# Attention and MoE scores in the two row halves of TensorE, without rounded or padded copies

## The chip, the cores and the metric

One Trainium2 chip, one NeuronCore of it. The metric is the time of one execution on the device in microseconds (us); where a kernel ran several times, the median is given. TensorE does matrix products into PSUM (eight banks); VectorE (DVE), ScalarE (ACT) and GpSimd (POOL) do the element-wise work; SyncE (SP) issues most of the transfers.

## The reference

Sliding-window attention (window 128) with a linear position bias is followed by a layer in which four single-head causal attentions act as experts, and each token mixes two of them. B, H, S, D = 8, 8, 576, 64; the model width is 512; there are 4 experts of head width 64.

```python
scores = scale * np.matmul(q, k.transpose(0, 1, 3, 2))
scores = np.where((rel >= 0) & (rel < 128), scores + bias[None], -1e9)
attn = softmax(scores); x = np.matmul(attn, v)          # x as (B, S, 512)
logits = x @ w_gate                                     # two of four experts, w = softmax over the two
for e in range(4):
    q = x @ wq[e]; k = x @ wk[e]; v = x @ wv[e]
    a = softmax(causal(scale * (q @ k.transpose(0, 2, 1))))
    out += gate[e] * ((a @ v) @ wo[e])
```

Inputs and output are fp32. In the kernel a product that has to be nearly fp32 is made in one of two ways: as an fp32 matmul, which the trace shows as two passes of each instruction, or as several matmuls on `float32r` (f32r) operands, a rounded number and the rest that rounding left (high and low part), each of which is one pass.

## The kernel before

**Work.** There are 32 attention groups: a batch of 8 with 4 pairs of heads each. For a group the scores of each head are made in blocks of 128 queries against the two key blocks that the window reaches (the first query block needs one), and the last 64 queries of both heads together as a tail (`attn_s`). VectorE merges the two key blocks under a mask, adds the bias and finds the row's extreme; ScalarE takes the exponential and sums; the blocks are scaled (`normalise`, on GpSimd or ScalarE), transposed on TensorE (`attn_t`), spread by VectorE and multiplied with v (`attn_pv`, `attn_pv_tail`: fp32, the two heads in the two column halves of TensorE). Per batch, x is then multiplied with the weights of q and k (`qkproj`: 12 f32r matmuls of 288 columns for each of 8 outputs) and of v and the gate (`vproj`); for each of two pairs of experts come causal scores in blocks of 128 queries against 128 to 512 keys (`moe_s`), a tail of 64 queries of both experts (`moe_s_tail`), scaling (`moe_norm`), transposes (`moe_t`), products with v (`moe_pv`, again two column halves) and the output product (`moe_wo`).

**Scores before.** Groups 0 to 5 (`n32` = 6) use the raw fp32 q and k: head 0 lies on partitions 0 to 63, head 1 on 64 to 127, and a matmul of 64 rows for each goes to its own row half of TensorE and its own bank (tile `e`). From group 6 on, a rounded copy `h` is brought in by a GpSimd transfer that casts (`load_hi`), the raw copy `r` by SyncE, and four GpSimd subtractions of 64 partitions x 576 make the low parts (`prep`, into `h` and `klA`); a block is then two f32r matmuls over all 128 rows, `s<-h` and `s<-klA,h`, for each head. The other half of the rows holds the low part of q, or padding. The MoE scores are the same: `QSm` holds the high part of q on one half of the rows and the low part on the other, `KHm` the high part of k on both (a transfer from SBUF to SBUF copies it over), `KLm` the low part beside zeros; an eviction of `qkproj` is two casts and two subtractions on 64 partitions each. A block is two matmuls, `ms<-KHm,QSm` and `ms<-KLm,QSm`, for each expert.

**Order.** Every operation is recorded first. A planner (`graph`, `ranks`, `schedule`, `plan`) then sets one fixed order for each engine: a list scheduler with a cost for each operation, ranks by the longest way to the end, and a table `off` in `K` that shifts the rank of each kind of tile in each phase. It charges for changing between row- or column-halved and full matmuls on TensorE, and puts a filling matmul (`warm`) where TensorE would be idle early on. On the chip each engine works through its list in order and waits where an operand is late.

**Buffers.** Scores lie in two PSUM banks (`ps_s`), transposes in two (`ps_t`), qk, v and o in two (`ps_a`), and the products with v in one bank each for attention and MoE.

**Names.** `s`: attention scores, `ms` and `msl`: MoE scores and their tail, `t`, `mt`, `mtl`: transposes, `x`, `xt`, `ma`, `mal`: products with v, `qk`, `v`, `o`: projections. All instructions carry line 1220, where the recorded list is issued; so they are told apart by tile.

Of the kernel before, what the change touches and what calls it, by code (L numbers as in the profile page):

```python
# [78 lines left out]

# [68 lines left out]
def _pairs(ops):  # L148
    two = {}
    for i in range(1, len(ops)):  # L150
        e, m, a, k = ops[i]
        if e != "tensor" or m != "matmul" or a[1].dtype != F32:
            continue
        x = a[0] if a[0].ap[0][1] == D else a[1]
        if x.ap[0][1] == D and x.offset // x.ap[0][0] >= D:
            assert ops[i - 1][0] == "tensor"
            two[i - 1] = i
    return two


def graph(ops, alt):
    n = len(ops)
    raw = _depend(ops)
    two = _pairs(ops)
    rep = list(range(n))
    for a, b in two.items():
        rep[b] = a
# [18 lines left out]
    alts = [[(ENG.index(o[0]), _cost(*o)) for o in alt.get(i, [ops[i]])] for i in nodes]  # L186
    port = [[_port(*o) for o in alt.get(i, [ops[i]])] for i in nodes]
# [4 lines left out]
    kind = []  # L192
    for i in nodes:
        e, m, a, k = ops[i]
        if e != "tensor":
            kind.append(0)
        elif i in two or (m == "matmul" and a[1].ap[0][1] == D):
            kind.append(3)
        elif m == "matmul" and a[1].dtype == F32R:
            kind.append(1)  # L200
        else:
            kind.append(2)
# [15 lines left out]
SWITCH = (150, 45)  # L218
# [5 lines left out]
def ranks(g):  # L224
# [15 lines left out]
    for i in reversed(topo):  # L240
        c = g["cost"][i] + (20 if g["kind"][i] == 3 else 0)
# [11 lines left out]
def schedule(g, rank, succ, setup=0.0, wt=0.5, bias=((0, 0, 0, 0, 0),) * 2, fill=(900, 60000, 9999), cw=6, hs=0):  # L253
    mode = 0
# [21 lines left out]
    while done < n:  # L276
# [97 lines left out]
def plan(ops, alt):  # L374
# [8 lines left out]
    for x in order:  # L383
# [6 lines left out]
        if i in g["two"]:  # L390
            out.append(ops[g["two"][i]])
# [13 lines left out]
class _Rec:  # L405
    def __init__(self):
# [3 lines left out]
        self.alt = {"hold": {}, "early": set()}  # L410
# [7 lines left out]
def attn_moe_kernel(ctx, tc, hd, rd, vd, wall, wo, mk, tb, tm, mt, ident, out):  # L418
# [4 lines left out]
    raw = ctx.enter_context(tc.tile_pool(name="raw", bufs=1))  # L423
# [49 lines left out]
    mkt = cp.tile([P, P + D], I32, name="mkt")  # L473
    tbt = cp.tile([P, NP_, 5, P], BF16, name="tbt")
# [14 lines left out]
    KLA = [cp.tile([P, 2, S], F32R, name=f"klA{k}") for k in range(2)]  # L489

    QW = S + TAIL
    HW = 2 * QW + 2 * S

    N32 = K["n32"]
    EK = QW

# [4 lines left out]
    def load_e(g):  # L501
# [806 lines left out]
```

## Time and profile before

| | |
|---|---|
| median of 3 runs | 582.44 us (580.57 to 585.34) |
| span of the profiled execution, first to last instruction | 583.1 us |
| TensorE busy, matmuls | 562.3 us |
| VectorE, ScalarE, GpSimd busy | 404.3, 420.0, 352.4 us |
| granted TensorE clock, mean | 0.991 |
| moved by DMA | 80.38 MB |

The profile gives no other time for the profiled execution than its span; it lies among the times of the runs, 0.7 us over their median. A matmul's busy time overlaps with that of the next one, since matmuls are pipelined; so what a matmul takes of TensorE is read here from one start to the next. An fp32 matmul stands in the trace as two records, its two passes.

### The profile page before, as it was taken

How to read it: one execution, taken by the hardware profiler on the slowest of the kernel's cores; microseconds unless marked ns; L12 is line 12 of the kernel's file. 1: busy time of each engine (PE TensorE's matmuls, PEld its weight loads, DVE VectorE, ACT ScalarE, POOL GpSimd, SP SyncE). 2: the span in 40 equal slices, each digit the busy share in tenths (PEclk: the TensorE clock that was granted, in tenths of full speed). 3: DMA queues.
4: the chain of work that ended last, by engine and by line, in shares of the span. 5: the costliest groups of instructions: out<-in, count | busy, mean ns of one | idle time of the engine just before them, and what ended most of it. 6: DMA issues, size and time to landing. Idle time of an engine off the chain costs nothing.

```text
span 583.1 us, 14004 instructions
## 1 busy us (share of the span) xinstructions
PE 562.3 (96%) x4565; PEld 477.2 (82%) x4565; DVE 404.3 (69%) x1784; ACT 420.0 (72%) x1456; POOL 352.4 (60%) x542
## 2 busy tenths in 40 slices
PE   7899999999998999999999999999999999999996
PEld 6667988789887888889888897888989898898764
DVE  3778788768775686766866687766887678555620
ACT  3776698858795686966978587776879667475853
POOL 3686687756766577666787557685679544143230
PEclk9999999999998999999999999999999999999998
DMA  9943575234743436453564446524465501210013
GB/s 203 310 133 128 166 248 174 85 119 150 225 149 82 147 118 215 168 154 106 164 209 145 123 142 200 198 73 120 151 206 168 166 24 35 82 39 2 21 56 108
DMA packets 29368, 80.38 MB, mean 138 GB/s; under 512 B 3440, under 2 KB 9072, under 8 KB 29296
## 3 DMA queue, kind: packets, MB, share of 16 engines
q1 hardware_dynamic: 21744, 45.44, 26.2%
q0 software_dynamic: 7232, 32.93, 17.3%
q10 hardware_dynamic: 320, 1.11, 0.8%
q8 instruction: 36, 0.59, 0.4%
q14 instruction: 36, 0.29, 0.2%
HBM read 65.32 MB, written 9.44 MB: 128 GB/s over the span
## 4 chain that ended last, share of the span: by engine, by line
PE 64%; POOL 10%; issue 7%; DMA 7%; DVE 6%; ACT 6%; ACTq 0%; SPq 0%; POOLq 0%; DVEq 0%
PE qk L1220 13%; PE v L1220 9%; PE s L1220 8%; PE o L1220 7%; PE x L1220 5%; PE ms L1220 5%; PE mt L1220 5%; PE t L1220 4%; PE ma L1220 4%; POOL h L1220 3%; ACT p L1220 3%; POOL klA L1220 2%; DMA e<-in_hd 2%; DMA h<-in_hd 2%; PE msl L1220 2%
## 5 line engine op out<-in xcount | busy, mean ns | idle before, releaser
L1220 ACT ACTIVATE p<-p,nm 128x128 f32<-128x128 f32 x288 | 113.1, 396 | 46.7 <-DVE nm L1220 45.5
L1220 PE MATMUL qk<-xh,WH 128*128 128x288 f32 x512 | 119.8, 312 | 0.7 <-DVE QSm L1220 0.5
L1220 POOL TENSOR_TENSOR h<-r,h 64x576 fp32r<-64x576 f32 x52 | 74.0, 1423 | 58.6 <-issue 26.0
L1220 POOL TENSOR_SCALAR p<-p,r 128x128 f32<-128x128 f32 x177 | 63.7, 373 | 55.7 <-DVE r L1220 31.3
L1220 POOL TENSOR_SCALAR mp<-mp,mr,w 128x128 f32<-128x128 f32 (+3 forms) x128 | 76.4, 608 | 34.2 <-DVE mr L1220 21.7
L1220 PEld LDWEIGHTS qk<-xh,WH 128*128 128x128 f32 x512 | 83.3, 189 | 8.1 <-PE ma L1220 2.4
L1220 DVE TENSOR_TENSOR pa<-t,tmt 128x512 f32<-128x512 f32 (+2 forms) x96 | 74.3, 776 | 19.4 <-ACT pa L1220 14.7
L1220 ACT ACTIVATE mp<-mp,mnm 128x256 f32<-128x256 f32 (+3 forms) x128 | 71.7, 560 | 18.3 <-DVE mnm L1220 17.0
L1220 DVE CUSTOM_DVE_ANT_0 p<-s,tbt 128x128 f32<-128x128 f32 x288 | 71.9, 286 | 5.4 <-PE t L1220 3.3
L1220 POOL TENSOR_TENSOR klA<-r,h 64x576 fp32r<-64x576 f32 x52 | 74.0, 1424 | 1.9
L1220 PE MATMUL qk<-xh,WL 128*128 128x288 f32 x256 | 70.8, 304 | 0.0
L1220 PE MATMUL s<-h 128*128 128x128 f32 (+2 forms) x260 | 70.0, 292 | 0.2 <-DVE nm L1220 0.2
L1220 DVE CUSTOM_DVE_ANT_0 mp<-ms,mtt 128x384 f32<-128x384 f32 (+3 forms) x128 | 59.9, 485 | 13.5 <-PE ms L1220 11.2
L1220 DVE COPY_PREDICATED s<-mkt,s 128x256 f32<-128x256 int32 (+2 forms) x160 | 50.2, 330 | 26.7 <-PE s L1220 25.8
L1220 PE MATMUL s<-klA,h 128*128 128x128 f32 (+2 forms) x260 | 68.5, 281 | 0.0
L1220 PE MATMUL v<-WH,xh 128*128 128x260 f32 x288 | 63.1, 304 | 3.6 <-DVE KLm L1220 3.5
L1220 PE MATMUL x<-pa,vt 128*64 128x256 f32 (+1 forms) x512 | 63.1, 360 | 0.0
L1220 PE MATMUL mt<-idt,mp 128*128 128x128 f32 x320 | 61.4, 276 | 0.2
L1220 PE MATMUL t<-idt,p 128*128 128x128 f32 x288 | 55.5, 277 | 3.7 <-POOL p L1220 2.1
L1220 ACT COPY mpt<-mt 128x384 f32<-128x384 f32 (+1 forms) x92 | 47.6, 527 | 14.2 <-PE mt L1220 9.5
L1220 ACT ACTIVATION_READ_ACCUMULATOR p<-p,nm 128x1 f32 x288 | 54.7, 190 | 0.0
L1220 PEld LDWEIGHTS s<-h 128*128 128x128 f32 x260 | 49.2, 191 | 6.3 <-issue 4.4
(121 smaller groups left out, 1366.7 us busy)
## 6 DMA issues: line engine op xcount, KB each, us to landing
h<-in_hd POOLq DMA_DIRECT2D x26, 1216.0 KB, 7.5
r<-in_rd SPq DMA_DIRECT2D x26, 576.0 KB, 4.0
vt<-in_vd SPq DMA_DIRECT2D x32, 320.0 KB, 3.6
out<-ot SPq DMA_DIRECT2D x32, 256.0 KB, 2.2
KHm<-KHm SPq DMA_DIRECT2D x64, 72.0 KB, 2.8
e<-in_hd SPq DMA_DIRECT2D x6, 304.0 KB, 8.1
wst<-in_wall SPq DMA_DIRECT2D x4, 386.0 KB, 6.4
e<-in_hd ACTq DMA_DIRECT2D x4, 272.0 KB, 6.0
```

The lines of the kernel that those rows point to most:

```text
L1220: getattr(getattr(tc.nc, e), m)(*a, **k)
```

## The change

- Attention scores use raw fp32 in the two row halves for all 32 groups; `load_hi`, `prep`, `klA`, the transfers of `h` and the padded layout go. The tail is one fp32 matmul on a small tile `q` that holds both heads' last queries.
- MoE scores use `QS` and `KS`, high and low part of q and k with expert 0 on the lower and expert 1 on the upper 64 partitions. A block is three terms (high x high, low x high, high x low), each a matmul of 64 rows for each expert, in the two row halves and two banks. An eviction of `qkproj` is one cast and one subtraction on 128 partitions; the copies of `KHm` go. For the tail a GpSimd product with a mask `bdt` makes `QB`; three matmuls of all rows for each half of the keys.
- `moe_s` makes both experts' blocks together, and so holds both score banks.
- The planner keeps pairs together (`glue`), has other costs, tells three kinds of matmul apart (full, row halves, column halves), and has a new table `off`; groups are loaded four ahead.

```diff
@@ planner
-SWITCH = (150, 45)
+SWITCH = 100
...
+def _kind(e, m, a):
+    if e != "tensor":
+        return 0
+    if m == "transpose":
+        return 1
+    if a[1].ap[0][1] != P:
+        return 2
+    return 3 if _free(a[1]) != P else 1
...
+    def glue(self, n):
+        self.alt["glue"].update(range(n + 1, len(self.ops)))
@@ load
-            r = raw.tile([P, 2 * S], F32, tag="r", name=f"r{g}")
...
-            nc.sync.dma_start(r, rd[b, p])
+            r = raw.tile([P, RW], F32, tag="r", name=f"r{g}")
...
+            nc.sync.dma_start(r[:D], hd[b, p, :D, :RW])
+            nc.sync.dma_start(r[D:], hd[b, p, D:, RW + P :])
+        q = raw.tile([P, P], F32, tag="q", name=f"q{g}")
+        nc.sync.dma_start(q, hd[b, p, :, RW : RW + P])
...
-        nc.gpsimd.dma_start(h.rearrange("p (a n) -> p a n", a=2), src)
...
-            ssub(kl[d, j, lo:hi], r[d, S + lo : S + hi], kh[j][d, lo:hi].bitcast(F32), sube(g))
...
-        ssub(t, x, t.bitcast(F32), sube(g))
@@ attn_s
-                nc.tensor.matmul(o, w, kh[h][:, S - TW :], start=(h == 0), stop=False)
-                nc.tensor.matmul(o, w, kl[:, h, S - TW :], start=False, stop=(h == 1))
+            nc.tensor.matmul(s[:, :TW], q, r[:, RW - TW :], start=True, stop=True)
...
-                nc.tensor.matmul(s[:, o : o + n], w, kh[h][:, k0 : k0 + n], start=True, stop=False)
-                nc.tensor.matmul(s[:, o : o + n], w, kl[:, h, k0 : k0 + n], start=False, stop=True)
+                d = r[D * h : D * h + D]
+                nc.tensor.matmul(ss[h][:, o : o + n], d[:, P * (i + h) : P * (i + h + 1)], d[:, k0 : k0 + n], start=True, stop=True)
+            nc.glue(n0)
@@ qkproj
-            act_copy(QS[0:D, pr, 0, sl], o[0:D], HALF)
-            act_copy(QS[D:P, pr, 1, sl], o[D:P], HALF)
-            dve_sub(QS[D:P, pr, 0, sl], o[0:D], QS[0:D, pr, 0, sl].bitcast(F32), HALF)
-            dve_sub(QS[0:D, pr, 1, sl], o[D:P], QS[D:P, pr, 1, sl].bitcast(F32), HALF)
...
-            nc.sync.dma_start(KH[D:P, pr, 0, sl].bitcast(F32), KH[0:D, pr, 0, sl].bitcast(F32))
-            nc.sync.dma_start(KH[0:D, pr, 1, sl].bitcast(F32), KH[D:P, pr, 1, sl].bitcast(F32))
...
+        t = QS if isq else KS
+        act_copy(t[:, pr, 0, sl], o, HALF)
+        dve_sub(t[:, pr, 1, sl], o, t[:, pr, 0, sl].bitcast(F32), HALF)
+        if isq and half == 1:
...
+            nc.gpsimd.tensor_tensor(QB[:, pr].rearrange("p a (j n) -> p a j n", j=2), q, w, mul)
@@ moe_s
-        s = ps_s.tile([P, 512], F32, tag="s", name=f"ms{b}_{pr}_{j}_{blocks[0]}")
+        ss = [ps_s.tile([P, 512], F32, tag="s", name=f"ms{b}_{pr}_{j}_{blocks[0]}") for j in range(2)]
...
-            nc.tensor.matmul(s[:, o : o + n], w, KH[:, pr, j, :n], start=True, stop=False)
-            nc.tensor.matmul(s[:, o : o + n], w, KL[:, pr, j, :n], start=False, stop=True)
+            for k, (x, y) in enumerate(TERMS):
+                for j in range(2):
+                    d = slice(D * j, D * j + D)
+                    nc.tensor.matmul(
+                        ss[j][:, o : o + n], QS[d, pr, x, P * i : P * (i + 1)], KS[d, pr, y, :n], start=(k == 0), stop=(k == 2)
+                    )
@@ moe_s_tail
-            for j in range(2):
-                w = QZ[:, pr, j, :]
-                nc.tensor.matmul(s[:, :HALF], w, KH[:, pr, j, sl], start=(j == 0), stop=False)
-                nc.tensor.matmul(s[:, :HALF], w, KL[:, pr, j, sl], start=False, stop=(j == 1))
+            for k, (x, y) in enumerate(TERMS):
+                nc.tensor.matmul(s[:, :HALF], QB[:, pr, x, :], KS[:, pr, y, sl], start=(k == 0), stop=(k == 2))
```

TensorE before, MoE scores of batch 4, first pair of experts, fourth query block of expert 0 (`ms4_0_0_3`), with what follows it; `s22_4` are scores of head 1 of attention group 22:

```order
L1220 MATMUL ms4_0_0_3_904<-KHm_106,QSm_102 128x512
L1220 MATMUL ms4_0_0_3_904<-KLm_107,QSm_102 128x512
L1220 MATMUL t21_0_898<-idt_87,p21_858 128x128
L1220 MATMUL mt3_1_1_1_891<-idt_87,mp3_1_1_845 128x128
L1220 MATMUL t21_0_898<-idt_87,p21_858 128x128
L1220 MATMUL mt3_1_1_1_891<-idt_87,mp3_1_1_845 128x128
L1220 MATMUL t21_0_898<-idt_87,p21_858 128x128
L1220 MATMUL mt3_1_1_1_891<-idt_87,mp3_1_1_845 128x128
L1220 MATMUL qk4_1_1_972<-xh16_718,WH_92 128x288
L1220 MATMUL s22_4_911<-h22_860 128x256
L1220 MATMUL s22_4_911<-klA0_100,h22_860 128x256
```

The same blocks of batch 4 on TensorE now, both experts (`ms4_0_0_3`, `ms4_0_1_3`):

```order
L1127 MATMUL t22_0_940<-idt_87,p22_904 128x128 x4
L1127 MATMUL ms4_0_0_3_937<-KSm_105,QSm_101 128x512
L1127 MATMUL ms4_0_1_3_938<-KSm_105,QSm_101 128x512
L1127 MATMUL ms4_0_0_3_937<-KSm_105,QSm_101 128x512
L1127 MATMUL ms4_0_1_3_938<-KSm_105,QSm_101 128x512
L1127 MATMUL ms4_0_0_3_937<-KSm_105,QSm_101 128x512
L1127 MATMUL ms4_0_1_3_938<-KSm_105,QSm_101 128x512
L1127 MATMUL qk4_3_0_989<-xh16_726,WH_93 128x288 x2
```

Two matmuls of one expert, all of the array's rows, among other work of full matmuls became six for two experts in a run of their own; before, expert 1's block 3 stands 86 rows further on.

TensorE before, the first scores of attention group 24 (`s24_0`), after them q and k projections and then a run in column halves (`x22`):

```order
L1220 MATMUL s24_0_957<-h24_925 128x128
L1220 MATMUL s24_0_957<-klA0_100,h24_925 128x128
L1220 MATMUL s24_0_957<-h24_925 128x256
L1220 MATMUL s24_0_957<-klA0_100,h24_925 128x256
L1220 MATMUL qk4_3_1_981<-xh18_782,WH_92 128x288
L1220 MATMUL qk4_3_1_981<-xh18_782,WL_93 128x288
```

And now, the first scores of group 24, both heads (`s24_0`, `s24_3`), and what stands around them:

```order
L1127 MATMUL qk4_3_0_989<-xh19_815,WL_94 128x288
L1127 MATMUL s24_0_967<-r24_820 128x128
L1127 MATMUL s24_3_968<-r24_820 128x128
L1127 MATMUL s24_0_967<-r24_820 128x256
L1127 MATMUL s24_3_968<-r24_820 128x256
L1127 MATMUL x22_947<-pa22_941,vt22_761 64x256 x2
L1127 MATMUL ma3_1_919<-mpt3_1_0_1_892,v23_710 64x384
```

Scores went from two full matmuls a block to a run in row halves for both heads; here the run in column halves follows directly.

GpSimd before, around the preparation of attention group 19 (`h19`, `klA1`):

```order
L1220 TENSOR_SCALAR p17_691<-p17_691,r17_0_706 128x128 x3
L1220 DMA h19_729<-in_hd 128x2x1216
L1220 TENSOR_SCALAR p17_691<-p17_691,r17_5_715 128x128 x3
L1220 TENSOR_TENSOR h19_729<-r19_722,h19_729 64x576 x2
L1220 TENSOR_TENSOR klA1_101<-r19_722,h19_729 64x576 x2
L1220 TENSOR_SCALAR p18_727<-p18_727,r18_0_739 128x128 x3
L1220 DMA h20_758<-in_hd 128x2x1216
```

GpSimd now, the scaling of group 17 and the start of that of group 18:

```order
L1127 TENSOR_TENSOR QBm_102<-QSm_101,bdt_89 128x256
L1127 TENSOR_SCALAR p17_700<-p17_700,r17_0_729 128x128
L1127 TENSOR_SCALAR p17_700<-p17_700,r17_5_730 128x128
L1127 TENSOR_SCALAR p17_700<-p17_700,r17_0_729 128x128
L1127 TENSOR_SCALAR p17_700<-p17_700,r17_5_730 128x128
L1127 TENSOR_SCALAR p17_700<-p17_700,r17_0_729 128x128
```

The transfer and the four subtractions of a group are gone from GpSimd; all of group 17's scaling stands there instead.

## Rows read from the trace of the kernel before

**Rows 1.** The page's first part: busy us, share of the span, instructions.

```profile
PE 562.3 (96%) x4565; PEld 477.2 (82%) x4565; DVE 404.3 (69%) x1784; ACT 420.0 (72%) x1456; POOL 352.4 (60%) x542
```

**Rows 2.** Windows: stretch, its length, busy us (instructions) by engine, clock, DMA share, GB/s.

```profile
180.00:250.00 70.00, 67.78 (x550) 58.49 (x549) 50.23 (x221) 51.00 (x179) 46.26 (x70) 0.98 0.47 149
250.00:325.00 75.00, 73.18 (x622) 63.93 (x622) 56.44 (x247) 56.02 (x196) 51.96 (x80) 1.00 0.49 151
```

**Rows 3.** Timeline of TensorE, 200 to 215 us: start, length, operation, tiles, shape, count.

```profile
201.84 0.28 PE L1220 MATMUL s<-h 128*128 128x256 f32 x1
201.96 0.28 PE L1220 MATMUL s<-klA,h 128*128 128x256 f32 x1
...
202.44 0.22 PE L1220 MATMUL s<-h 128*128 128x128 f32 x1
202.50 0.28 PE L1220 MATMUL s<-klA,h 128*128 128x128 f32 x1
202.62 0.34 PE L1220 MATMUL s<-h 128*128 128x256 f32 x1
...
203.48 0.29 PE L1220 MATMUL qk<-xh,WH 128*128 128x288 f32 x1
203.61 0.42 PE L1220 MATMUL qk<-xh,WL 128*128 128x288 f32 x2
...
214.63 0.40 PE L1220 MATMUL ms<-KHm,QSm 128*128 128x512 f32 x1
214.87 0.39 PE L1220 MATMUL ms<-KLm,QSm 128*128 128x512 f32 x1
```

**Rows 4.** Timeline of TensorE, 9 to 18 us: raw fp32 scores, two row halves, then tails.

```profile
9.07 0.60 PE L1220 MATMUL s<-e 64*128 64x256 f32 x4
...
9.71 0.82 PE L1220 MATMUL s<-e 64*128 64x128 f32 x8
...
17.36 0.49 PE L1220 MATMUL s<-e,tails 128*128 128x192 f32 x2
17.69 0.27 PE L1220 MATMUL t<-idt,p 128*128 128x128 f32 x1
```

**Rows 5.** Timeline of TensorE at runs in halves, at 41 and 86 us.

```profile
40.83 0.39 PE L1220 MATMUL x<-pa,vt 128*64 128x128 f32 x4
41.15 0.70 PE L1220 MATMUL s<-e 64*128 64x256 f32 x4
41.78 0.53 PE L1220 MATMUL qk<-xh,WH 128*128 128x288 f32 x2
42.15 0.30 PE L1220 MATMUL qk<-xh,WL 128*128 128x288 f32 x1
...
85.84 0.29 PE L1220 MATMUL qk<-xh,WL 128*128 128x288 f32 x1
86.06 0.65 PE L1220 MATMUL x<-pa,vt 128*64 128x256 f32 x4
86.64 0.66 PE L1220 MATMUL t<-idt,p 128*128 128x128 f32 x4
87.05 0.42 PE L1220 MATMUL ms<-KHm,QSm 128*128 128x384 f32 x1
```

**Rows 6.** Groups of instructions: busy us, mean ns, idle before and what ended it.

```profile
L1220 POOL TENSOR_TENSOR klA<-r,h 64x576 fp32r<-64x576 f32 x52 | 74.0, 1424 | 1.9
L1220 POOL TENSOR_TENSOR h<-r,h 64x576 fp32r<-64x576 f32 x52 | 74.0, 1423 | 58.6 <-issue 26.0 <-DMA h<-in_hd 21.4 <-ACT QSm L1220 4.3
...
L1220 DVE TENSOR_TENSOR KLm<-qk,KHm 64x288 fp32r<-64x288 f32 x64 | 28.3, 452 | 4.8 <-ACT KHm L1220 4.0
```

**Rows 7.** Waits of TensorE: what waited for what, us in total, times, longest.

```profile
PE v L1220 <- DVE KLm L1220: 3.5, 3, 1.8
PE t L1220 <- POOL p L1220: 2.1, 2, 1.8
```

More of the change, by code (lines that the diff above doesn't have):

```diff
@@ L145, in _depend @@
     return pred
[L148 to L158, printed above, removed]
 def graph(ops, alt):
@@ L163, in graph @@
     raw = _depend(ops)
-    two = _pairs(ops)
     rep = list(range(n))
-    for a, b in two.items():
-        rep[b] = a
+    parts = {}
+    for i in range(1, n):
+        if i in alt["glue"]:
+            assert ops[i][0] == ops[i - 1][0] == "tensor"
+            rep[i] = rep[i - 1]
+            parts.setdefault(rep[i], []).append(i)
     nodes = [i for i in range(n) if rep[i] == i]
@@ L186, in graph @@
     alts = [[(ENG.index(o[0]), _cost(*o)) for o in alt.get(i, [ops[i]])] for i in nodes]
+    for x, i in enumerate(nodes):
+        if i in parts:
+            alts[x] = [(0, sum(_cost(*ops[j]) for j in [i] + parts[i]))]
     port = [[_port(*o) for o in alt.get(i, [ops[i]])] for i in nodes]
@@ L191, in graph @@
     dma = [(_bytes(ops[i][2][0]) if ops[i][1] == "dma_start" else 0) for i in nodes]
[L192 to L202, printed above, removed]
+    kind = [_kind(*ops[i][:3]) for i in nodes]
     cat = [re.match(r'[A-Za-z]*[a-z]*', ops[i][2][0].tensor.name).group(0) + ops[i][0][0] for i in nodes]
@@ L240, in ranks @@
     for i in reversed(topo):
-        c = g["cost"][i] + (20 if g["kind"][i] == 3 else 0)
+        c = g["cost"][i] + (20 if g["kind"][i] > 1 else 0)
         for j, w in succ[i]:
@@ L389, in plan @@
         out.append(next(o for o in q if o[0] == ENG[g["on"][x]]))
-        if i in g["two"]:
-            out.append(ops[g["two"][i]])
+        for j in g["parts"].get(i, ()):
+            out.append(ops[j])
     return out
@@ L488, in attn_moe_kernel @@
     MSM = [cp.tile([P, 19], F32, name=f"msm{k}") for k in range(2)]
[L489 to L495, printed above, removed]
+    RW = 2 * S + TAIL
+    KO = S + TAIL
     def load_vt(g):
@@ L572, in sube @@
-    def sube(g):
-        return ("vector", "gpsimd", None)[int(K["sub"][min(g, len(K["sub"]) - 1)])]
     def warm():
-        s = ps_s.tile([P, 4 * P], F32, tag="s", name="warm")
         z = ps_a.tile([P, 512], F32, tag="m" if K["M"] else "a", name="warm2", bufs=K["M"] or K["A"])
-        nc.alt["fill"] = ("tensor", "matmul", (z[:, :256], QZ[:, 0, 0, :], QZ.rearrange("p a b n -> p (a b n)")[:, :256]), dict(start=True, stop=True))
-        for _ in range(K["wu"]):
-            nc.tensor.matmul(s[:, :256], QZ[:, 0, 0, :], QZ.rearrange("p a b n -> p (a b n)")[:, :256], start=True, stop=True)
@@ L647, in s_tile @@
+        for h in range(2):
+            wrap(ss[h], 2 * u)
+            blocks(g, ss[h], part[h])
     def s_tile(g, u):
@@ L964, in moe_pv @@
             )
+        nc.glue(len(nc.ops) - 2)
         if c == NQ - 1:
@@ L1017, in wload @@
     def wload(c):
-        if c < 4 and K["wv"]:
+        if c in (2, 3):
+            w = raw.tile([P, RW], F32, tag="r", name=f"wst{c}")
+        elif c < 4:
             w = m1.tile([P, NQ + 1, E * D], F32, tag="v2", name=f"wst{c}", bufs=2).rearrange("p a n -> p (a n)")
@@ L1172, in attn_moe_kernel @@
     nc.sync.dma_start(tbt[:, 1], tb[:, 1])
-    load_e(2)
+    load(2)
     load_vt(1)
     nc.sync.dma_start(tbt[:, 2:], tb[:, 2:])
-    load_e(3)
-    wload(0)
-    wload(1)
+    load(3)
+    load_vt(2)
+    for c in range(4):
+        wload(c)
+    load_vt(3)
+    load(4)
+    wload(4)
+    load(5)
     aseq, marks = attn_units()
```

256 lines of the change are left out of this document (85 added, 171 removed).

## Prediction

> **What bounds the kernel now.** I read the page's first part, then the windows, then the timeline of TensorE (PE), then its waits. The page has matmuls busy for 96% of the span and no other engine over 72% [rows 1]. The windows say the same of stretches in mid-kernel: TensorE 67.78 of 70 us and 73.18 of 75, VectorE at 72 and 75% [rows 2]. So TensorE's queue sets the pace, and a change is worth what it takes out of that queue, plus the waits in it that it removes, less the waits that it brings. Busy shares can't say what a matmul costs, since the matmuls overlap; the distance from one start to the next does. The reader is to see four distances. An f32r matmul over all rows takes 0.12 us at 256 columns (201.84 to 201.96), 0.13 at 288 (203.48 to 203.61) and 0.24 at 512; two at 128 columns take 0.06 and 0.12, 0.18 together [rows 3]. At 384 columns I put 0.18, an estimate half way between 256 and 512. A pass of raw fp32 scores in the two row halves takes 0.215 us at 256 columns for both heads together (9.07 to 9.71 are six records, three passes for two heads, 0.64), about 0.11 at 128, an estimate by half; a tail of 192 columns over all rows takes 0.33 for its two passes (17.36 to 17.69) [rows 4].
>
> **Columns taken out of TensorE, attention.** 26 groups change; the first six are as before. Before, a head takes 0.18 + 6 x 0.12 = 0.90 us, two heads 1.80, and the tail is four matmuls of 192 columns, which I put at 0.115 each, between 0.11 and 0.12 (near the 256): 0.46. Sum 2.26. After, per group one pair of 128 and three of 256 columns, two passes each: 2 x 0.11 + 6 x 0.215 = 1.51, and one tail 0.33: 1.84. Gain 0.42 x 26 = 10.9 us. So raw fp32 in halves costs TensorE scarcely less than two f32r matmuls: half the rows, but two passes at half the speed.
>
> **Columns, MoE.** Before, an expert's blocks take 0.18 + 0.24 + 0.36 + 0.48 = 1.26 us, both 2.52, the tail 8 x 0.13 = 1.04. After, if two f32r matmuls of 64 rows run side by side as the fp32 ones do, three pairs per block: 3 x (0.09 + 0.12 + 0.18 + 0.24) = 1.89, where 0.09 lies between the 0.06 and 0.12 of 128 columns, and the tail is 6 x 0.13 = 0.78. Gain 0.89 x 16 = 14.2 us. The trace of before has no f32r matmul in a half. Its bounds are side by side (the above) and one after the other: 1.89 more for each of 16, 30.2 us, a loss of 16.0. I take side by side, since the halves of raw scores and those of the products with v both do so in this trace [rows 4, 5]. Columns together: -25.1 us.
>
> **Switches put in.** A run in halves costs TensorE something at both ends. At 41 us a run in row halves stands between one in column halves and a projection. Two passes of 128 before it take 0.32 instead of 0.22 (+0.10), the run's two passes 0.63 instead of 0.43 (+0.20), the two projections behind it 0.37 instead of 0.26 (+0.11): 0.41 for two switches. At 86 us a run in column halves stands between a projection and transposes: 0.22 for 0.13 (+0.09), 0.58 for 0.43 (+0.15), and four transposes 0.41, of which I count +0.06: 0.30 [rows 5]. So a switch costs 0.15 to 0.20, and at least the 0.10 of one end alone; I take 0.17. Counted in TensorE's order, with three kinds (full, row halves, column halves), the kernel before changes kind 160 times, the new one 315 times. The order above shows why: blocks that were full matmuls among full matmuls became runs of their own. 155 x 0.17 = 26.4 us. The Trainium skill, TensorEngine Tiling (Array Packing), Key Properties, says that a change of tiling mode drains the engine, and gives no price. By that rule, with a price of the 0.10 at one end alone, it would be 15.5 and the sum 8.3 us lower than I put it; the rows, where the first pass and the next full matmul are late too, bear out the dearer reading.
>
> Some of these switches fall where TensorE waits anyway, and a drain in a wait is free. It is idle 1.8 us of 75 in mid-kernel [rows 2], a small share; I let a tenth be hidden: 23.8 us stay. TensorE's own work so comes to -25.1 + 23.8 = -1.3 us, next to nothing.
>
> **Other engines.** GpSimd loses the 104 subtractions, 2 x 74.0 us, and its casting transfers; VectorE loses half of its subtractions at evictions (64 of 452 ns instead of 128, about 28 us), and ScalarE half of its casts likewise [rows 6]. GpSimd takes on scaling in return, as the order shows, and 16 products for `QB`; these lie beside TensorE's work. None of this is on the path by itself. It counts by the waits of TensorE that it ends: v and qk wait for the eviction that `KLm` closes, 3.5 us in three waits, and transposes wait for GpSimd's scaling, 2.1 us [rows 7]. With one cast and one subtraction in place of two and two, and GpSimd free of 5.7 us in one block per group, I let both go. The longest of these waits, 1.8 us, stands ahead of a stretch where the granted clock was 0.98 over 70 us, the lower of its two levels (1.2 GHz) for a part: 0.02 x 70 = 1.4 us [rows 2, 7], which goes too. Together -7.0. Bounds: 0, if other operands are then late by as much, and about -12, if the same again goes in the weight loads ahead of those matmuls. I take the 7.0 that the rows name.
>
> At nothing I cost: the transfers (mean DMA share 0.47 to 0.49 in mid-kernel [rows 2]; they get fewer, and groups come four ahead; if they came late, a group's scores would wait), the removed copies of `KHm` (issued by SyncE; their landing is not among the long waits), and the first six groups, whose loads keep their sizes.
>
> **Sum.** 583.1 - 1.3 - 7.0 = 574.8 us by the profiled execution; the median of the runs lies 0.7 lower: 574.1, so 574. From no change a measurement can tell about 1%: faster is below 576.6, slower above 588.3.
>
> **Rivals.** All in the runs' median.
> - *More is hidden.* The trace has TensorE waiting in many short waits; if half of the new switches fall into such waits, 13.2 us of 26.4 stay, and it ends at 583.1 - 25.1 + 13.2 - 7.0 - 0.7 = 563.5. For it: every run in halves also waits for operands. Against: the 96% of [rows 1].
> - *Waits come back.* TensorE does no less work, so what is late next takes the place of the waits removed, and no switch is hidden: 583.1 - 25.1 + 26.4 - 0.7 = 583.7, no change. For it: VectorE and ScalarE, at 69 and 72%, lose only some 28 us each or a little more.
> - *Weight loads in turn.* If the two loads of a pair in halves don't run together, each pair is bound by two loads of 0.11 (the step from the second 128-column matmul to the next, 0.12 [rows 3], is such a load): 0.22 for 128, 256 and 384 columns. That is 3 x (0.13 + 0.10 + 0.04) = 0.81 more, x 16 = 13.0: 587. The Trainium skill, TensorE: Matmul & The Clock Gate, LDWEIGHTS, says that a load takes as long for 32 rows as for 128, by its columns. Against it: passes of raw scores, 128 columns in both halves, take about 0.11 with two loads each [rows 4].
> - *Not side by side.* f32r in halves runs one after the other: 30.2 us more, 604. Against it only the fp32 rows.
> - *Both score banks at once, slower than before.* A pair of heads or experts now fills both banks of `ps_s`, so TensorE can't write the next scores while VectorE reads the last; the time of a turn (TensorE, VectorE, back) stands open each time. There are 28 x 2 such turns of attention and 16 x 3 of MoE, 104. If other work stands behind them in the queue for all but 0.15 us of each, 15.6 us are lost: 590. From 0.14 us a turn on it decides, since 104 x 0.14 = 14.6 is the way from 574 to slower. For it: VectorE, busy 75% [rows 2], must be free just then. Against: much other work is queued between the pairs, as the projections in the order show.
>
> **How the numbers follow.** The forecast has 0.37, its own range 567 to 582 (switches at 0.15 to 0.20, waits from 3 to 12), of which 0.28 lies below 576.6 and 0.09 above. More hidden 0.20, waits come back 0.23, loads in turn 0.03, not side by side 0.05, score banks 0.12. Faster: 0.28 + 0.20 = 0.48. Within 1%: 0.09 + 0.23 + 0.03 = 0.35. Slower: 0.05 + 0.12 = 0.17. The range takes in most of the case with more hidden and of the score banks' and leaves out 604: 557 to 594.
>
> **What would show it.** In the new trace, a pair of MoE matmuls at 512 columns should start a few ns apart and the next pair 0.24 us later; 0.48 would mean one after the other. First passes in runs should be some 0.1 us longer than later ones, and so each full matmul behind a run. TensorE's waits for the evictions of qk should be gone, and none for scaling be long. If VectorE's waits for `s` and `ms` grow and TensorE waits at scores, the banks are the cause. The forecast is wrong if a switch costs under 0.1 us, or if the waits of TensorE grow.

## The result and the profile after

The changed kernel takes 561.75 us (median of 4 runs, 561.70 to 563.63) against 581.53 us (4 runs, 580.57 to 585.34): ratio 0.9655, interval 0.9599 to 0.9712, 3.4% faster. Forecast were 574.1 us and 8.3 us of gain; measured are 19.8. The time lies in the range given (557 to 594), the gain is more than twice the forecast one.

The page's first part of the changed kernel, as [rows 1]:

```profile
PE 552.2 (99%) x4599; PEld 440.1 (79%) x4599; DVE 370.1 (66%) x1713; ACT 365.0 (65%) x1296; POOL 217.9 (39%) x494
```

TensorE is busy for 99% of a shorter span. GpSimd falls by 134 us, ScalarE by 55 and VectorE by 34. The page's chain of waits, first before, then after:

```profile
PE 64%; POOL 10%; issue 7%; DMA 7%; DVE 6%; ACT 6%; ACTq 0%; SPq 0%; POOLq 0%; DVEq 0%
```

```profile
PE 96%; DMA 2%; ACTq 0%; issue 0%; ACT 0%
```

Before, 36% of the chain lay outside TensorE's matmuls, 10% of it on GpSimd; after, 4%, and none on GpSimd. The windows of the changed kernel (stretch, its length, busy us and instructions by engine, clock, DMA share, GB/s), as [rows 2]:

```profile
180.00:250.00 70.00, 70.00 (x599) 55.94 (x599) 48.51 (x226) 47.55 (x171) 26.61 (x63) 1.00 0.29 79
250.00:325.00 75.00, 75.00 (x641) 61.52 (x637) 53.17 (x242) 49.38 (x180) 29.73 (x72) 1.00 0.30 83
```

The whole run in two stretches, TensorE alone, before and then after:

```profile
0.00:30.00 30.00, 24.34 (x174) 0.95 0.99 261
30.00:577.00 547.00, 537.37 (x4392) 1.00 0.42 132
```

```profile
0.00:30.00 30.00, 27.63 (x205) 1.00 0.90 244
30.00:554.00 524.00, 524.00 (x4394) 1.00 0.26 73
```

Idle time of TensorE fell from 5.7 to 2.4 us in the first 30 us and from 9.6 to nothing behind them; the granted clock is 1.00 (the upper level, 2.4 GHz) where it was 0.95 in the first 30 us and 0.98 in one stretch of [rows 2]. All waits of TensorE that the trace of the changed kernel names, as [rows 7]:

```profile
PE warm L1127 <- DVE QBm L1127: 1.6, 1, 1.6
PE s L1127 <- DVE s L1127: 0.5, 1, 0.5
PE s L1127 <- DMA e<-in_hd: 0.3, 1, 0.3
```

Both rows of [rows 7] are gone. Before, the same view has thirteen rows with 14.7 us together; these three have 2.4.

Idle time is not all. A matmul's record is longer (0.28 us) than the distance to the next start (0.12), so the next can be late by 0.16 without an idle gap. I therefore counted from all of TensorE's starts, for each kernel three sums. *Columns*: the usual distances of all matmuls by shape. *Turns*: what the runs in halves, with the first full matmul behind each, take beyond that. *Late*: what all other full matmuls, from 30 to 577 us, take beyond it. Changes of kind are counted in the traces; before's are 158 there, for the prediction's 160.

| | columns | turns | late | changes of kind | span |
|---|---|---|---|---|---|
| before | 518.3 | 32.8 | 24.5 | 158 | 583.1 |
| after | 492.0 | 60.4 | 3.2 | 315 | 559.6 |
| difference | -26.3 | +27.6 | -21.3 | +157 | -23.5 |

With the first 30 us (idle time 3.3 less) the differences make -23.3, which is the span's difference. By this split TensorE's own work is as long as before, and the gain is its waits. But only the sum is fixed by the span; the split hangs on what is taken for a usual distance, and not all that comes late has waited. In before's scores the first matmul of 256 columns behind a pair of 128 takes 0.17 (205.39 to 205.56), the second 0.13:

```profile
205.28 0.27 PE L1220 MATMUL ms<-KLm,QSm 128*128 128x128 f32 x1
205.39 0.34 PE L1220 MATMUL ms<-KHm,QSm 128*128 128x256 f32 x1
205.56 0.28 PE L1220 MATMUL ms<-KLm,QSm 128*128 128x256 f32 x1
205.69 0.22 PE L1220 MATMUL s<-klA,h 128*128 128x128 f32 x1
```

The trace has 71 such places from 30 us on, 0.05 us over the usual 0.12 each, 3.7 us together; with these matmuls they are gone from the changed kernel. How much of *late* did wait is for e5 to say. The span's difference is larger than that of the medians, 19.8: a run of the changed kernel takes 2.1 us more than its span (561.71 and 559.6), by which the profiled execution before took about 585.2, as long as the slowest of the runs shown.

The timeline of the changed kernel where MoE scores run in row halves, as [rows 5]:

```profile
254.85 1.03 PE L1127 MATMUL t<-idt,p 128*128 128x128 f32 x8
255.81 0.80 PE L1127 MATMUL ms<-KSm,QSm 64*128 64x384 f32 x6
256.54 0.50 PE L1127 MATMUL v<-WH,xh 128*128 128x260 f32 x2
256.88 0.28 PE L1127 MATMUL v<-WL,xh 128*128 128x260 f32 x1
...
266.69 0.60 PE L1127 MATMUL t<-idt,p 128*128 128x128 f32 x4
267.21 0.97 PE L1127 MATMUL ms<-KSm,QSm 64*128 64x512 f32 x6
268.11 0.81 PE L1127 MATMUL qk<-xh,WH 128*128 128x288 f32 x4
```

Six f32r matmuls of 512 columns take 0.90 us to the next start, 267.21 to 268.11. One after the other they would take 6 x 0.24 = 1.44; side by side 3 x 0.24 = 0.72 and what the turn adds. The records of a pair start 3 to 4 ns apart. The v matmuls behind the run at 255.81 show the turn's end: 0.34 for two where the same kernel has 0.24 elsewhere.

### The profile page after: what moved, and what is told of

Read it like the earlier page. It is cut to its first block, busy times and chain, and to the rows that moved or that the text cites. A ratio compares the mean times of both kernels' runs of the same rounds, so it can differ in the third digit from the quotient of the medians.

```text
span 559.6 us, 13643 instructions
## 1 busy us (share of the span) xinstructions
PE 552.2 (99%) x4599; PEld 440.1 (79%) x4599; DVE 370.1 (66%) x1713; ACT 365.0 (65%) x1296; POOL 217.9 (39%) x494
## 4 chain that ended last, share of the span: by engine, by line
PE 96%; DMA 2%; ACTq 0%; issue 0%; ACT 0%
PE qk L1127 19%; PE s L1127 12%; PE v L1127 10%; PE x L1127 10%; PE o L1127 9%; PE ms L1127 7%; PE mt L1127 7%; PE ma L1127 7%; PE t L1127 6%; DMA e<-in_hd 2%; PE msl L1127 2%; PE mal L1127 2%; PE xt L1127 2%; PE mtl L1127 1%; PE warm L1127 1%; ACTq L1127 0%
## 5 line engine op out<-in xcount | busy, mean ns | idle before, releaser
L1127 POOL TENSOR_SCALAR p<-p,r 128x128 f32<-128x128 f32 x262 | 92.6, 378 | 149.7 <-DVE r L1127 81.4
L1127 ACT ACTIVATE mp<-mp,mnm 128x256 f32<-128x256 f32 (+3 forms) x128 | 71.1, 559 | 24.3 <-DVE mnm L1127 23.5
L1127 DVE COPY_PREDICATED s<-mkt,s 128x128 f32<-128x128 int32 (+2 forms) x160 | 47.3, 331 | 39.1 <-PE s L1127 38.8
L1127 PE MATMUL qk<-xh,WL 128*128 128x288 f32 x256 | 71.6, 305 | 0.0
L1127 DVE CUSTOM_DVE_ANT_0 mp<-ms,mtt 128x128 f32<-128x128 f32 (+3 forms) x128 | 57.6, 485 | 21.1 <-PE ms L1127 20.8
L1127 DVE CUSTOM_DVE_ANT_0 p<-s,tbt 128x128 f32<-128x128 f32 x288 | 69.0, 285 | 1.3 <-PE t L1127 0.4
L1127 ACT COPY mpt<-mt 128x384 f32<-128x384 f32 (+1 forms) x95 | 49.1, 530 | 25.5 <-PE mt L1127 23.5
L1127 PE MATMUL s<-r 64*128 64x128 f32 (+1 forms) x448 | 58.2, 377 | 0.0
L1127 PE MATMUL mt<-idt,mp 128*128 128x128 f32 x320 | 51.9, 276 | 0.0
L1127 PEld LDWEIGHTS v<-WH,xh 128*128 128x128 f32 x288 | 45.7, 189 | 5.4 <-issue 3.1
L1127 PEld LDWEIGHTS qk<-xh,WL 128*128 128x128 f32 x256 | 46.0, 189 | 0.8 <-issue 0.6
L1127 PEld LDWEIGHTS s<-r 64*128 64x128 f32 x448 | 33.9, 186 | 15.7 <-issue 5.8
L1127 PEld LDWEIGHTS x<-pa,vt 128*64 128x64 f32 x512 | 31.7, 137 | 17.6 <-issue 4.2
```

The lines of the kernel that those rows point to most:

```text
L1127: getattr(getattr(tc.nc, e), m)(*a, **k)
```

## Experiments

Two theories at the start. LIGHTER: the waits went because GpSimd, VectorE and ScalarE have less to do, so operands come in time. ORDER: they went because the planner, with a third kind, other costs and a new table, made another order. Later two on the turns: TURNS, a change of kind costs TensorE by itself; LATE, the runs in halves merely wait for operands. Ratios are to the kernel before, run beside. Differences from the changed kernel are between medians of separate comparisons; taken from the ratios they come out 0.2 to 2.3 us smaller.

**e1, attention alone.** All groups take raw fp32 scores; the MoE part, planner, costs and table are those of before.

```diff
-'n32': 6
+'n32': 32
```

> The kernel before with raw fp32 attention scores for all 32 groups, MoE part and planner as before, its order made anew by the old planner. TensorE changes kind 321 times instead of 160 in this order. By the sizes of the prediction: columns -10.9 us, switches 161 x 0.17 = +27.4, so +16.5 before any wait. Theory LIGHTER (TensorE's waits go because GpSimd's preparation, the evictions of qk and the copies are less work): with GpSimd freed of 148 us some 10 to 15 us of waits go, 583 to 588 us. Theory ORDER (the waits go because the new planner's costs and table make an order in which every operand is early): the old planner keeps the waits, 596 to 602 us.

593.44 us, ratio 1.0126 (1.0075 to 1.0176).

**e2, MoE alone.** Three-term MoE scores with their evictions; attention, planner and table as before.

```diff
-            act_copy(KH[0:D, pr, 0, sl], o[0:D], HALF)
-            act_copy(KH[D:P, pr, 1, sl], o[D:P], HALF)
...
+        act_copy(t[:, pr, 0, sl], o, HALF)
+        dve_sub(t[:, pr, 1, sl], o, t[:, pr, 0, sl].bitcast(F32), HALF)
```

> The kernel before with the three-term MoE scores in two row halves, the smaller evictions and the masked tail; attention (rounded copies from group 6 on) and planner as before, its order made anew by the old planner. 294 changes of kind on TensorE instead of 160. Columns -14.2 us, switches 134 x 0.17 = +22.8, so +8.6 before any wait. LIGHTER: the waits for evictions go, about 5 us or a little more, 582 to 586 us. ORDER: 588 to 594 us.

589.84 us, ratio 1.0113 (1.0076 to 1.0149). Each half alone makes the kernel 1% slower. e1 lies between the two theories, e2 in ORDER's range. By the count each has nearly all the turns of the two together (58.3 and 59.7 us of 60.4; the traces have 267 and 290 changes of kind, for 321 and 294 expected) for a part of the columns (510.1 and 506.3), and lateness falls only to 13.4 and 15.4. So the halves don't add up: together they have few more changes of kind than one. Both halves under the old planner were not tried.

**e3, less on GpSimd, order of before.** The planned order of before is kept, word for word, but 96 of the 104 subtractions are not issued (the low parts `klA` and `h` of groups from 8 on keep old values).

```diff
     for e, m, a, k in seq_:
+        t = a[0].tensor.name
+        if m == "tensor_tensor" and len(a) > 3 and re.match(r"(klA|h)\d", t):
+            if int(re.match(r"[a-z]*(\d+)", a[1].tensor.name).group(1)) >= 8:
+                continue
```

> The kernel before in the same order on every engine, but the 96 subtractions on GpSimd for attention groups 8 to 31 are left out (the low parts of q and k of those groups are not made, so scores there use old values): 137 us less on GpSimd, nothing else changed. LIGHTER: waits go, 567 to 573 us. ORDER: 579 to 582 us, no change, since TensorE's operands come from where they came.

576.95 us, ratio 0.9841 (0.9791 to 0.9890). Between the two. TensorE's work is the same to the instruction, and late falls from 24.5 to 17.0. TensorE's waits, as [rows 7]:

```profile
PE t L1224 <- POOL p L1224: 2.0, 2, 1.6
PE t L1224 <- DVE ALTm L1224: 1.7, 4, 0.4
PE warm L1224 <- DVE QZm L1224: 1.6, 1, 1.6
PE o L1224 <- ACT AHm L1224: 1.5, 5, 0.4
...
PE qk L1224 <- DVE KLm L1224: 0.2, 1, 0.2
```

The wait of `v` for `KLm`, an eviction on VectorE, is gone though only GpSimd was relieved; the wait for GpSimd's scaling, which I had put down to these subtractions, stands. VectorE is busy for 404.5 us, as before (404.3), so GpSimd's work does not slow it; what that work does is hold operands back. One thing e3 can't tell: with a subtraction the scores' wait for it goes too. For that e4 adds work that nothing waits for.

**e4, the changed kernel with GpSimd loaded again.** Ahead of the scaling of each group from 5 to 30 four subtractions of 64x576 on spare tiles.

```diff
+            for x in range(4):
+                h = slice(D * (x % 2), D * (x % 2) + D)
+                tc.nc.gpsimd.tensor_tensor(wk2[h], wk[h], wk[h], sub)
```

> The changed kernel in the same order, with four subtractions of 64 x 576 on GpSimd put in ahead of the scaling of each of the attention groups 5 to 30, on tiles of their own (104 in all, 148 us more on GpSimd; nothing depends on them). LIGHTER: TensorE's waits come back by 10 us or more, 572 to 582 us. ORDER: the order has room for it, 561 to 565 us.

580.67 us, ratio 0.9940 (0.9903 to 0.9977), as LIGHTER said: 18.9 us over the changed kernel, with the same order and work on TensorE. Late is 11.2 for 3.2, and the runs in halves wait too (turns 71.6 for 60.4). What was added, TensorE's longest waits, the chain, and TensorE alone from 100 to 180 us:

```profile
L1136 POOL TENSOR_TENSOR wk<-wk 64x576 f32<-64x576 f32 x104 | 118.8, 1143 | 6.2
```

```profile
PE x L1137 <- DVE pa L1137: 7.5, 5, 4.0
PE mt L1137 <- POOL MPL L1137: 3.9, 1, 3.9
```

```profile
PE 85%; POOL 8%; DVE 4%; DMA 1%; issue 1%; ACT 0%; ACTq 0%; SPq 0%; POOLq 0%
```

```profile
100.00:180.00 80.00, 73.50 (x576) 0.94 0.24 65
```

GpSimd is busy for 58% of that span, no bound by its share, and yet 118.8 us on it cost 18.9 us at the end. A part of that is the clock: it fell to its lower level (1.2 GHz) twice in this stretch, each time right behind one long wait of TensorE (3.9 us for `MPL`, 4.0 us for `pa`). By the mean of 0.94, 0.06 x 80 makes up to 4.8 us, an estimate; the changed kernel has 1.00 there.

**e5, lighter all round, order of before.** As e3, and from batch 1 on half of the casts and subtractions at the evictions of q and k (those on the upper 64 partitions) and 56 of the 64 copies of `KHm` are not issued either; their tiles keep old values.

```diff
+        q = re.match(r"qk(\d+)_", src)
+        if q and int(q.group(1)) >= 1 and a[0].offset // a[0].ap[0][0] >= D:
+            continue
+        if m == "dma_start" and "KHm" in t:
+            done_k[0] += 1
+            if done_k[0] > 8:
+                continue
```

> The kernel before in the same order on every engine, lighter on three: the 96 subtractions on GpSimd for groups 8 to 31 left out as in the run with less GpSimd work, and of batches 1 to 7 half of the casts and subtractions of each eviction of q and k and the copies of KHm left out (so scores use old values). TensorE's work is the same, 160 changes of kind. The run without the subtractions gained 9 us. LIGHTER: the waits for evictions go too, 4 to 6 us more, 567 to 571 us. ORDER: what is left of the waits belongs to the order, 574 to 578 us.

568.57 us, ratio 0.9763 (0.9731 to 0.9795), as LIGHTER said: 13.3 us by lighter engines alone (56 of the transfers went with them), in before's order and with before's matmuls. TensorE from 30 us to near the end, where before it was idle for 9.6 us:

```profile
30.00:561.00 531.00, 529.49 (x4385) 1.00 0.38 128
```

Idle 1.5 us; late 9.6, for 24.5 before and 17.0 in e3. So 14.9 us of lateness end with lighter engines, 1.4 of them by the clock of [rows 2], which is 1.00 here. What is left need not be waiting: the slow matmuls of 256 columns behind those of 128 stand here at 72 places. Of the 21.3 in the table 6.4 are thus not shown to be waits. The start is another matter; TensorE in the first 30 us of e5, and then of the changed kernel with an empty table (e7 below):

```profile
0.00:30.00 30.00, 23.55 (x182) 1.00 0.99 260
0.00:30.00 30.00, 25.02 (x188) 1.00 0.88 238
```

Idle 6.5 and 5.0 us, for 5.7 before and 2.4 in the changed kernel: lighter engines by themselves don't shorten the start, and without the table most of what it gained is lost again.

**e6, the changed kernel with before's table and the planner's weights of before.**

```diff
-'off': {...}, 'setup': 8474.7813, 'wt': -0.0565, 'bv': 2057.0354, ...
+'off': {...}, 'setup': 8000, 'wt': -0.5, 'bv': 36, ...
```

> The changed kernel with the planner's table off and its weights (setup, wt, bv, ba, bp, hs, bz) as in the kernel before; operations, costs and kinds as after. TensorE changes kind 358 times instead of 315. The order is another. By switches alone 43 x 0.17 = +7.3 over the changed kernel's 561.75. LIGHTER: about 569 us, waits near zero as after. ORDER: TensorE's waits of 10 to 15 us come back on top, 576 to 590 us.

577.10 us, ratio 0.9908 (0.9876 to 0.9940): 15.3 us over the changed kernel. The time is in ORDER's range, but not by its mechanism: late is only 5.1; the rest is 358 changes of kind (turns 71.0, 10.6 more) and 2.9 us of filler matmuls more. A bad order costs turns here more than waits.

**e7, the changed kernel with an empty table.**

```diff
-'off': {'AHTmsb': -100147, ...}
+'off': {}
```

> The changed kernel with the planner's table off left empty, so that ranks are the longest way to the end alone; all else as after. 294 changes of kind instead of 315, which alone would be 21 x 0.17 = -3.6. LIGHTER: 558 to 566 us. ORDER: waits of 10 us and more, 570 to 590 us.

565.91 us, ratio 0.9723 (0.9681 to 0.9764), as LIGHTER said: the table is worth 4.2 us (late 6.5 for 3.2, idle in the first 30 us 5.0 for 2.4).

**e11, the kernel before with an empty table.** The same edit to the kernel before.

> The kernel before with an empty table of offsets: the planner orders it anew, with the instructions and costs of before; 165 changes of kind for 160, so 1 us. ORDER (the re-made order is what took the waits away): an order from the planner alone would do about as well as with the lighter engines, 560 to 572 us. LIGHTER (before's waits are those of its GpSimd and evictions, which no order hides): 576 to 592 us.

583.08 us, ratio 1.0005 (0.9976 to 1.0033), as LIGHTER said. Another order, late 24.0 for 24.5, but other names in the waits of TensorE:

```profile
PE mtl L1220 <- DVE pa L1220: 2.3, 2, 1.2
PE s L1220 <- POOL h L1220: 1.8, 1, 1.8
...
PE t L1220 <- POOL p L1220: 1.2, 3, 0.6
```

So the two waits of [rows 7] were not the places where the engines were too slow; they were where this order showed it. With the heavier engines two orders give the same lateness, with the lighter ones three give 3.2 to 6.5 us.

**e8 and e12, fewer changes of kind.** A step behind the planner puts a run in halves off to the next of its kind, where less than 1 us (e8, 291 changes) or 0.6 us (e12, 308) of full matmuls stands between and none of it needs the run.

```diff
+    order, _ = gather(g, order, 1000)
```

> The changed kernel with a step behind the planner: a run in halves on TensorE is put off to the next run of its kind where less than 1 us of other matmuls stands between and none of them needs it. Same operations, 291 changes of kind instead of 315. By 0.17 us a switch 24 x 0.17 = 4.1 us less, 557 to 558 us, if the runs that are put off make nobody wait; 561 to 565 us if a switch costs little or the later runs are waited for.

> The changed kernel with runs in halves put off to the next run of their kind where less than 0.6 us stands between: 308 changes of kind for 315. PRICE: 7 x 0.17 = 1.2 us less, 560 to 561.5 us. WAITS (what follows a run in halves is wanted at once, as with the limit of 1 us): 563 to 567 us.

568.14 us (0.9752, 0.9720 to 0.9783) and 563.74 us (0.9666, 0.9615 to 0.9716). e8 missed, e12 came out as WAITS said: 24 and 7 changes less bring nothing; e12's ratio can't be told from the changed kernel's. TensorE's waits of e8:

```profile
PE s L1183 <- DVE nm L1183: 1.9, 2, 1.0
PE warm L1183 <- DVE QBm L1183: 1.6, 1, 1.6
PE t L1183 <- ACT p L1183: 1.5, 3, 1.2
```

The softmax behind the scores (`nm`, `p`) is late, by 3.4 us in these rows; what makes up the rest of e8's 6.4 us is open. No version tried beats the changed kernel.

**e9 and e10, the price of a turn.** 64 matmuls of zeros are put into the midst of 64 projection chains of the changed kernel, at the same places, once over 64 rows and once over 128.

```diff
+        if i in pick:
+            tc.nc.tensor.matmul(a[0][:, :128], zz[:64], a[2][:64, :128], start=False, stop=False)
```

> The changed kernel, and 64 matmuls more: one in the midst of each of 64 projection chains of full-tile matmuls, of zeros (nothing is added to the sums), 64 rows by 128 columns, so that TensorE turns to the row half and back 64 times more. Its operands are long there. TURNS (a change of kind costs 0.17 us, whatever is late): 64 x 0.11 of columns and 64 x 0.34 to 0.40 for the round trips, 29 to 33 us over the changed kernel, 590 to 595 us. LATE (what the runs in halves show beyond their columns is operands that come late): as the kernel with 128 rows, 564 to 570 us.

> The same 64 matmuls at the same places, but of 128 rows: no change of kind. Both theories: 64 x 0.06 to 0.11 us of columns, 4 to 7 us over the changed kernel, 565 to 569 us. What is asked is the difference from the kernel with 64 rows: TURNS 22 to 26 us, LATE under 5 us.

590.33 us (590.26 to 590.49) and 568.79 us (568.73 to 569.05); ratios 1.0117 (1.0055 to 1.0178) and 0.9748 (0.9698 to 0.9797). The difference is 21.5 us, just under the 22 to 26 of TURNS, for 128 changes of kind between full and row halves: 0.168 us each, with operands long there. LATE is out. One such place in the timeline, with 64 rows and then with 128:

```profile
212.30 0.43 PE L1142 MATMUL qk<-xh,WH 128*128 128x288 f32 x2
212.66 0.32 PE L1144 MATMUL qk<-xh,zz 64*128 64x128 f32 x1
212.91 0.40 PE L1142 MATMUL qk<-xh,WL 128*128 128x288 f32 x1
213.15 0.43 PE L1142 MATMUL qk<-xh,WH 128*128 128x288 f32 x2
```

```profile
205.85 0.43 PE L1142 MATMUL qk<-xh,WH 128*128 128x288 f32 x2
206.12 0.22 PE L1144 MATMUL qk<-xh,zz 128*128 128x128 f32 x1
206.18 0.35 PE L1142 MATMUL qk<-xh,WL 128*128 128x288 f32 x1
206.37 0.43 PE L1142 MATMUL qk<-xh,WH 128*128 128x288 f32 x2
```

From the first to the last start 0.85 us against 0.52: the turn there and back costs 0.33. It is spread: 0.09 from the two projections to the added matmul, 0.19 from that to the next, 0.05 from there on. "Changing tiling mode (not just tile) drains the TensorE", says the Trainium skill, TensorEngine Tiling (Array Packing), Key Properties; these two runs agree and put 0.168 us to it.

## Why the prediction was right and wrong

The step that failed is the sum of the waits: "I let both go ... Together -7.0", with the bound "about -12". e5 ends 14.9 us of lateness by lighter engines alone (the 1.4 of the clock is in both), more than the bound. Two terms more were put at nothing or too low. The start, whose loads I held to be the same, has 3.3 us less idle time. And 6.4 us of the table's lateness are not shown to be waits; up to 3.7 of them are the slow matmuls of 256 columns, which the column sum has at 0.12 and the trace at 0.17 (205.39 above). Together 24.6 in place of 7.0. With 3.8 us of turns more than put and 1.2 us of columns saved beyond the forecast, that is the 15 us by which the span came out below 574.8. In the gain by the medians it is 11.5 us: the 0.7 us between profile and median was wrong too, as the profiled execution before took some 3.7 us more than the median.

Why the waits were so far off:
- I priced waits by the names in [rows 7], two of thirteen rows. All thirteen make no more than 14.7 us, since they hold idle time alone, and a late start under an overlapping record leaves none. The starts that I measured columns with would have given more.
- I asked which wait the removed instruction ended. e3 and e11 show that the name is no cause: with the subtractions gone the wait of `v` for `KLm` goes and that for scaling stays, and in another order other names come up with the same sum. A relieved engine takes lateness out everywhere: 7.5 us by GpSimd's subtractions (24.5 to 17.0), 7.4 more by evictions and copies (to 9.6).
- "None of this is on the path by itself" is against the page's chain of before, shown above: 10% of it lay on GpSimd. The changed kernel has none there, and e4, which loads GpSimd again, has 8%.

The other steps:
- *Columns*, -25.1: measured -26.3, right but for the slow matmuls just named, which the count holds under *late*. f32r in halves runs side by side, so the rival with 604 us falls. "Different tiles can execute LdWeights and Matmul in parallel", of the Trainium skill (TensorEngine Tiling (Array Packing), Key Properties), agrees with starts 3 to 4 ns apart.
- *Weight loads in turn*, 587 us: no. Pairs of 128 columns start 0.109 us apart, the time of one load and not the 0.22 of two; I had put 0.09, which is 0.06 us a block too little.
- *Switches*, 155 x 0.17 = 26.4: measured +27.6 from the starts for 157, and 0.168 each by e9 and e10. The tenth that I let be hidden was not; with hardly a wait left there is little to hide it in. *More is hidden*, whose 563.5 us is nearest to the measured time, is so the wrong mechanism with nearly the right sum.
- *Waits come back*, 583.7 us: no. TensorE's work is hardly less, but the lateness did not move elsewhere, as VectorE and ScalarE fell to 66 and 65% and GpSimd to 39%.
- *Score banks*, 590 us: no. The wait for `s` is 0.5 us, and none for `ms`.
- *What would show it*: pairs a few ns apart, no waits for evictions of q and k, none for scaling, all as said. The next pair at 512 columns follows after 0.23, for 0.24.

LIGHTER so carries most of the gain: 13.3 of the 19.8 us come in before's order with before's matmuls (e5), and 18.9, clock included, are lost again when GpSimd alone is loaded as before (e4). The other 6.5 us are not told apart by a run; the shorter start, which goes with the table (e7), and the slow matmuls, which go with the f32r scores, are part of them. What the fewer transfers (46.00 MB for 80.38) give by themselves was not tried.

## What to carry to other kernels

Where one engine is nearly always busy, don't price its waits by the named rows: take the distances from start to start, less the usual distance of each shape, and sum them; then leave work out of an unchanged order to see how much of the sum was waiting. Work on an engine at 40 to 60% is not free if it delays operands: here a fifteenth (e3, 9.2 us by its ratio for 96 x 1.42 us) to a sixth (e4) of it came out at the end. And count changes of matmul kind before and after an edit: 157 more of them ate a saving of 26 us whole.

## What the hardware showed that I had not expected

A change of kind on TensorE, between full matmuls and a row half, costs 0.168 us though nothing is late (e9, e10), and its price is spread over three matmuls, so that no single one looks slow. Fewer changes are no gain if a chain behind a run waits for it (e8: 24 less, 6.4 us slower). And a long wait can cost more than itself: in e4 the granted clock fell to its lower level right behind idle times of 3.9 and 4.0 us, which makes up to 4.8 us more, an estimate.
